# Attention backward on one Trainium2 core: the scores of the next step beside the dP pair, dV/dK quads that lag two units and dQ quads eight, in a fixed order

## The chip, the cores and the metric

The kernel runs on one core of one Trainium2 chip. The metric is the device time of the whole kernel in microseconds (us); each figure is the median of three or four runs of one version. "Unit" below means the smallest piece of the attention backward stage: 4 heads, 128 queries, 512 keys. The stage has 512 units. A "half step" handles two of the four heads. In the profiles PE is TensorE's matmuls, PEld its weight loads, DVE VectorE, ACT ScalarE, POOL GpSimd, and SPq the queue on which SyncE issues transfers. SBUF and PSUM are the on-chip memories; matmuls write to PSUM. "dsT" is the tile that holds dS transposed; "the ring" below is the cycle in which the dQ quads free a dsT buffer, transposes fill it, these free dS buffers for the next multiplies, and later dQ quads follow.

## The reference, cut to what matters

The program is one transformer block (adaLN conditioning, attention, squared-ReLU MLP), forward and backward, on 2048 tokens, 512 channels, 32 heads of 16 channels. Only this part and its derivative matter here:

```python
scores = jnp.einsum('bhqd,bhkd->bhqk', q, k) * Dh ** (-0.5)
p = _softmax(scores, axis=-1)
o = jnp.einsum('bhqk,bhkd->bhqd', p, v)
```

For the derivative, the kernel recomputes E = exp(scores), computes dP = dO V^T with the softmax correction folded into an extra row, multiplies dS = E * dP, and then accumulates dV from E, dK from dS, and dQ from dS transposed.

## The kernel before

Each head occupies 32 of the 128 partitions, so the score and dP matmuls (S and dP below) are **row-tiled**: a matmul uses 32 rows of the PE array at row position 0, 32, 64 or 96. The accumulating matmuls come as **quads**, one matmul per head, and are **column-tiled**: all 128 rows, 32 columns each (16 for dV).

```python
ework = ...tile_pool(name="phIe", bufs=3)
tpool = ...tile_pool(name="phIt", bufs=2)                 # dsT: dS transposed, one block of 4 units
psu = ...tile_pool(name="psIu", bufs=3, space=PSUM)       # S and dP share three buffers
psa = ...tile_pool(name="psIa", bufs=1, space=PSUM)

def score_pair(u, pair):
    ...
    if pair == 0:
        bst[u] = (ework.tile([P, 4, 512], BF, name="E_u", tag="E_u"),
                  ework.tile([P, 4, 512], BF, name="dS_u", tag="dS_u", bufs=4))
    E_u, dS_u = bst[u]
    psS = psu.tile([P, 2, 512], F32, name="psS_u", tag="pu")
    for hi in range(2):
        r = 32 * (2 * pair + hi)
        PE.matmul(psS[:, hi, :], ..., tile_position=(r, 0))               # S
    ACT.activation(E_u[:, 2 * pair:2 * pair + 2, :], psS[:], AF.Exp, scale=SCALE)
    psD = psu.tile([P, 2, 512], F32, name="psD_u", tag="pu")
    for hi in range(2):
        r = 32 * (2 * pair + hi)
        PE.matmul(psD[:, hi, :], ..., tile_position=(r, 0))               # dP
    DVE.tensor_tensor(dS_u[:, 2 * pair:2 * pair + 2, :], psD[:], E_u[...], ALU.mult)

def transpose_unit(u):
    if qi == 0:
        dqt[hg, qc, kc] = tpool.tile([P, 16, 512], BF, name="dsT", tag="dsT")
    SP.dma_start(out=dqt[hg, qc, kc][:, :, qi * P:(qi + 1) * P], in_=..., transpose=True)

def kv_quads(u): ...      # 4 matmuls with dS (dK), 4 with E (dV), into accVK
def dq_quad(b, kt): ...   # 4 matmuls with dsT, into dqacc; needs all four transposes of its block

LAG = 6
for u in range(NU + LAG + 4):
    if u < NU:
        ...                                   # load_head two blocks ahead
        score_pair(u, 0)
    if 1 <= u <= NU:
        kv_quads(u - 1)
    if u < NU:
        score_pair(u, 1)
        transpose_unit(u)
    v = u - LAG - 3
    if 0 <= v < NU:
        dq_quad((hg, qc, kc), qi)
```

The text of the loop is not the order that runs: a scheduler orders the instructions of each engine when the program is built.

## Time and profile before

| | before |
|---|---|
| whole kernel, median | 5007.97 us |
| attention backward, first exp to end of last dQ matmul | 2144 us |
| per unit | 4.19 us |
| granted TensorE clock in the stage | 0.61 |

The first view is the table of one stretch of time, here the stage. Its columns are the stretch, its length, then the busy time of each engine with the number of its instructions, the granted clock, the DMA share and GB/s.

```profile
core 0: us, PE busy (x) PEld busy (x) DVE busy (x) ACT busy (x) POOL busy (x), PEclk, DMA share, GB/s
2574.00:4720.00 2146.00, 1944.39 (x10234) 368.38 (x10233) 1222.26 (x1024) 1100.73 (x1185) 152.85 (x110) 0.61 0.73 136
```

PE is busy 91% of the stage, while DVE and ACT are busy 57% and 51%. One should not conclude that PE's arithmetic is the bound. The Trainium skill, "Trainium Kernel Development and Optimization", Performance Expectations, warns that matmul busy time is a bad metric for how close a kernel is to its roofline, because matmuls are pipelined.

The groups of instructions by line show the duration of one operation (second number) and how long its engine sat idle just before it, with what ended that idle time:

```profile
L716 DVE TENSOR_TENSOR dS_u<-psD_u,E_u 128x1024 bf16<-128x1024 f32 x1024 | 1222.3, 1222 | 965.6 <-ACT E_u L710 780.2
L710 ACT ACTIVATE E_u<-psS_u 128x1024 bf16<-128x1024 f32 x1024 | 1018.6, 1023 | 886.3 <-PE psS_u L708 881.4
...
L714 PE MATMUL psD_u<-iv,ido 32*128 32x512 bf16 x2048 | 643.3, 540 | 107.7 <-ACT E_u L710 91.9
...
L708 PE MATMUL psS_u<-ik,iq 32*128 32x512 bf16 x2048 | 601.6, 532 | 22.5 <-ACT E_u L710 14.8
...
L762 PE MATMUL dqacc<-dsT,KS_tok 128*32 128x512 bf16 x2048 | 427.9, 605 | 12.5 <-DMA dsT<-dS_u 9.8
```

ACT needs 2 x 1.02 us per unit and DVE 2 x 1.22 us, well under 4.19 us. ACT waits for scores, DVE waits for exp. The list of waits (who waited for whom, total us, times, longest) says the same for 2700 to 4700 us:

```profile
ACT E_u L710 <- PE psS_u L708: 829.6, 552, 3.4
DVE dS_u L716 <- ACT E_u L710: 683.0, 486, 3.2
```

The timeline shows how PE works at the low clock. Columns: start, duration, engine, line, operation, tiles, count, and in brackets the idle time before it and its releaser.

```profile
3405.05 0.61 PE L736 MATMUL accVK<-dS_u,qz_14655 128*32 128x512 bf16 x2
...
3405.60 0.60 PE L708 MATMUL psS_u<-ik,iq 32*128 32x512 bf16 x1
...
3406.13 0.61 PE L736 MATMUL accVK<-dS_u,qz_14655 128*32 128x512 bf16 x2
...
3406.14 1.03 PE L739 MATMUL accVK<-E_u,dOs_tok 128*16 128x512 bf16 x4
...
3407.10 0.60 PE L708 MATMUL psS_u<-ik,iq 32*128 32x512 bf16 x1
3407.10 1.02 PE L714 MATMUL psD_u<-iv,ido 32*128 32x512 bf16 x2
3407.74 1.02 ACT L710 ACTIVATE E_u<-psS_u 128x1024 bf16<-128x1024 f32 x1 [2.36 <-PE psS_u L708]
...
3408.06 0.61 PE L762 MATMUL dqacc<-dsT,KS_tok 128*32 128x512 bf16 x1
...
3408.60 0.61 PE L708 MATMUL psS_u<-ik,iq 32*128 32x512 bf16 x2
...
3408.79 1.23 DVE L716 TENSOR_TENSOR dS_u<-psD_u,E_u 128x1024 bf16<-128x1024 f32 x1 [1.94 <-ACT E_u L710]
```

Groups of one tiling kind start 0.54 us apart when they hold one set of matmuls (3405.05, 3405.60, 3406.13) and 0.96 us apart when they hold two serial sets (3406.14 to 3407.10). A lone score matmul at 3405.60 costs the same 0.54 us as a full set would. S and dP on the same row tiles need two sets (3407.10 to 3408.06). The Trainium skill, "TensorEngine Tiling (Array Packing)", Key Properties, says that changing the tiling mode drains TensorE; the trace agrees, with about 0.11 us per group beyond 0.43 us per set.

### The profile page before, as it was taken

What the parts mean: (1) busy time and instruction counts of PE and PEld (TensorE: products, weight loads), DVE (VectorE), ACT (ScalarE), POOL (GpSimd) and SP (SyncE); (2) the same over time, 40 slices, a digit from 0 to 9 for tenths busy, and PEclk for the clock granted to TensorE, in tenths of its full rate; (3) what the DMA queues carried; (4) which work ended last, traced back from release to release, by engine and by line L of the source; (5) the groups of instructions that cost most, each with busy time, mean ns of one, the idle gap of its engine ahead of it and who ended that gap; (6) DMA issues with size and microseconds to landing.
All of it is one profiled execution on the core that took longest, in us unless ns stands there. A gap on an engine that the chain in (4) does not pass through costs nothing.

```text
span 5010.0 us, 48266 instructions
## 1 busy us (share of the span) xinstructions
PE 4158.7 (83%) x18556; PEld 1052.9 (21%) x18629; DVE 2069.8 (41%) x3264; ACT 2232.8 (45%) x2462; POOL 274.0 (5%) x282
## 2 busy tenths in 40 slices
PE   4789999999997872866579999998989999989766
PEld 1222222222222321322221111111111111111122
DVE  7610000000004752720336555555555555555473
ACT  0058888888884000000025555545554554555411
POOL 2000000000000000001310000010000000000000
PEclk7865555555555886966855565666565655666687
DMA  3220000000001243365467867777686877677513
GB/s 110 82 79 9 9 1 9 9 9 8 2 1 42 110 129 90 89 204 173 133 148 132 159 127 150 128 134 143 125 153 123 153 124 147 127 134 130 123 56 92
DMA packets 1212437, 489.34 MB, mean 98 GB/s; under 512 B 1144611, under 2 KB 1174823, under 8 KB 1210669
## 3 DMA queue, kind: packets, MB, share of 16 engines
q1 hardware_dynamic: 1189550, 455.84, 41.5%
q0 software_dynamic: 6144, 28.32, 1.9%
q10 hardware_dynamic: 16512, 2.10, 0.3%
q8 instruction: 146, 2.39, 0.2%
q14 instruction: 85, 0.70, 0.0%
HBM read 124.35 MB, written 80.37 MB: 41 GB/s over the span
## 4 chain that ended last, share of the span: by engine, by line
PE 33%; ACT 8%; DVE 5%; DMA 3%; issue 3%; SPq 1%; POOL 0%; ACTq 0%; DVEq 0%; POOLq 0%
PE psS_u L708 8%; PE accVK L736 8%; ACT E_u L710 7%; PE psD_u L714 6%; PE dqacc L762 5%; PE accVK L739 4%; DVE dS_u L716 3%; DMA dsT<-dS_u 1%; SPq L919 1%; DMA stld<-stok_st 0%; DVE dh1acc L831 0%; DVE dqkv_tok L823 0%; DMA out_dram<-w2blk 0%; ACT vktmp L747 0%; POOL dOs_tokpad L595 0%
## 5 line engine op out<-in xcount | busy, mean ns | idle before, releaser
L716 DVE TENSOR_TENSOR dS_u<-psD_u,E_u 128x1024 bf16<-128x1024 f32 x1024 | 1222.3, 1222 | 965.6 <-ACT E_u L710 780.2
L710 ACT ACTIVATE E_u<-psS_u 128x1024 bf16<-128x1024 f32 x1024 | 1018.6, 1023 | 886.3 <-PE psS_u L708 881.4
L302 ACT ACTIVATE ET<-psST 128x1024 bf16<-128x1024 f32 x1024 | 1046.5, 1024 | 228.4 <-PE psST L299 226.3
L714 PE MATMUL psD_u<-iv,ido 32*128 32x512 bf16 x2048 | 643.3, 540 | 107.7 <-ACT E_u L710 91.9
L299 PE MATMUL psST<-qt_sb,kt_sb 32*128 32x512 bf16 x2048 | 658.3, 603 | 17.3 <-DMA kt_sb<-KtP 17.3
L306 PE MATMUL oacc<-ET,vaug 128*32 128x512 bf16 x2048 | 626.1, 604 | 45.9 <-ACT ET L302 4.5
L708 PE MATMUL psS_u<-ik,iq 32*128 32x512 bf16 x2048 | 601.6, 532 | 22.5 <-ACT E_u L710 14.8
L309 DVE COPY ostage<-oacc 128x512 f32<-128x512 f32 x32 | 22.1, 692 | 1083.7 <-PE oacc L306 1083.7
L739 PE MATMUL accVK<-E_u,dOs_tok 128*16 128x512 bf16 x2048 | 462.9, 554 | 0.0
L762 PE MATMUL dqacc<-dsT,KS_tok 128*32 128x512 bf16 x2048 | 427.9, 605 | 12.5 <-DMA dsT<-dS_u 9.8
L736 PE MATMUL accVK<-dS_u,qz_14655 128*32 128x512 bf16 x1024 | 316.8, 543 | 35.5 <-DVE dS_u L716 35.3
L736 PE MATMUL accVK<-dS_u,qz_14654 128*32 128x512 bf16 x1024 | 303.7, 557 | 26.8 <-DVE dS_u L716 26.7
L708 PEld LDWEIGHTS <-iq 32*128 32x128 bf16 x2048 | 126.1, 96 | 663.8 <-issue 650.3
L306 PEld LDWEIGHTS <-vaug 128*32 128x32 bf16 x2048 | 151.7, 102 | 466.1 <-issue 437.5
L570 ACT ACTIVATE w1blk<-aw_0_13090 128x512 bf16<-128x512 f32 x1 | 0.6, 597 | 556.2 <-PE aw_0_13090 L566 556.2
L748 POOL TENSOR_TENSOR dVKacc<-dVKacc,vktmp 128x512 f32<-128x512 f32 x96 | 121.3, 1264 | 1910.0 <-ACT vktmp L747 1910.0
L714 PEld LDWEIGHTS <-ido 32*128 32x128 bf16 x2048 | 144.2, 100 | 331.6 <-issue 309.3
L299 PEld LDWEIGHTS <-kt_sb 32*128 32x128 bf16 x2048 | 111.4, 99 | 478.0 <-issue 478.0
L490 PE MATMUL pds<-gfT,w2T 128*128 128x512 bf16 x219 | 54.4, 400 | 109.6 <-DVE dzT L493 79.5
L736 PEld LDWEIGHTS <-qz_14655 128*32 128x32 bf16 x1024 | 59.1, 99 | 312.4 <-issue 311.9
L736 PEld LDWEIGHTS <-qz_14654 128*32 128x32 bf16 x1024 | 56.1, 99 | 295.8 <-issue 295.8
L262 PE MATMUL ppad<-xn1T,wpadT 128*128 128x512 bf16 x376 | 99.1, 409 | 21.7 <-DVE stagep L265 16.2
(1253 smaller groups left out, 2931.6 us busy)
## 6 DMA issues: line engine op xcount, KB each, us to landing
dzld<-dztok_st POOLq DMA_DIRECT2D x32, 448.0 KB, 3.7
dzld<-dztok_st SPq DMA_DIRECT2D x32, 448.0 KB, 3.6
dsT<-dS_u SPq DMA_TRANSPOSE x512, 4.3
rT_st<-rT SPq DMA_DIRECT2D x4, 1792.0 KB
rtok_st<-rtok SPq DMA_DIRECT2D x16, 448.0 KB, 2.5
stok_st<-stok SPq DMA_DIRECT2D x16, 448.0 KB
rTb<-rT_st SPq DMA_DIRECT2D x4, 1792.0 KB
rtokb<-rtok_st SPq DMA_DIRECT2D x16, 448.0 KB, 4.0
```

Source lines behind the costliest of these rows:

```text
L262: PE.matmul(pp[:], wpadT[:, ic, which, hg, :], h1T[:, ic, qc * 512:(qc + 1) * 512], start=(ic == 0), stop=(ic == DC - 1))
L299: PE.matmul(ps[:, hi, :], kt_sb[32 * hq:32 * hq + 32, kt * P:(kt + 1) * P], qt_sb[32 * hq:32 * hq + 32, qc * 512:(qc + 1) * 512], start=Tr ...
L302: ACT.activation(ET[:, 2 * pair:2 * pair + 2, :], ps[:], AF.Exp, scale=SCALE)
L306: PE.matmul(oacc[32 * hq:32 * hq + 32, :], lhsT, ET[:, hq, :], start=(kt == 0), stop=(kt == TT - 1), tile_position=(0, 32 * hq), skip_grou ...
L708: PE.matmul(psS[:, hi, :], st["q"][r:r + 32, qt * P:(qt + 1) * P], st["k"][r:r + 32, kc * 512:kc * 512 + 512], start=True, stop=True, tile ...
L710: ACT.activation(E_u[:, 2 * pair:2 * pair + 2, :], psS[:], AF.Exp, scale=SCALE)
L714: PE.matmul(psD[:, hi, :], st["do"][r:r + 32, qt * P:(qt + 1) * P], st["v"][r:r + 32, kc * 512:kc * 512 + 512], start=True, stop=True, til ...
L716: DVE.tensor_tensor(dS_u[:, 2 * pair:2 * pair + 2, :], psD[:], E_u[:, 2 * pair:2 * pair + 2, :], ALU.mult)
L736: PE.matmul(acc[32 * hq:32 * hq + 32, :], st["qz"][:, qt, hq, :], dS_u[:, hq, :], start=(qi == 0), stop=False, tile_position=(0, 32 * hq), ...
L739: PE.matmul(acc[32 * hq:32 * hq + DH, :], dOs_tok[:, qt, (hg * 4 + hq) * DH:(hg * 4 + hq + 1) * DH], E_u[:, hq, :], start=False, stop=(qi ...
L748: POOL.tensor_tensor(dst, dst, tmp[:], ALU.add)
L762: PE.matmul(acc[32 * hq:32 * hq + 32, :], KS_tok[:, kc * 4 + kt, h * DH:h * DH + 32], tT[:, hq * 4 + kt, :], start=(kc == 0 and kt == 0), ...
```

## The change

Its intent: fix the instruction order of PE, ACT and DVE by hand. In each half step j, issue the scores S(j) next to dP(j-1), which sits on the other two row tiles, so that all four row tiles work at once; then one whole kind of quads. dV/dK quads lag two units, dQ quads eight (one and nine in the text before). A fourth E buffer pays for the longer lag.

```diff
-                bst[u] = (ework.tile([P, 4, 512], BF, name="E_u", tag="E_u"),
+                bst[u] = (ework.tile([P, 4, 512], BF, name="E_u", tag="E_u", bufs=4),
                           ework.tile([P, 4, 512], BF, name="dS_u", tag="dS_u", bufs=4))
 ...
             ACT.activation(E_u[:, 2 * pair:2 * pair + 2, :], psS[:], AF.Exp, scale=SCALE)
+
+        def dp_pair(u, pair):
 ...
             psD = psu.tile([P, 2, 512], F32, name="psD_u", tag="pu")
 ...
-        for u in range(NU + LAG + 4):
-            if u < NU:
-                ...
-                score_pair(u, 0)
-            if 1 <= u <= NU:
-                kv_quads(u - 1)
-            if u < NU:
-                score_pair(u, 1)
-                transpose_unit(u)
-            v = u - LAG - 3
-            if 0 <= v < NU:
-                hg, qc, kc, qi = units[v]
-                dq_quad((hg, qc, kc), qi)
+        with tc.manual_schedule(engines={PE.engine, ACT.engine, DVE.engine}):
+            for j in range(2 * NU + 18):
+                u = j // 2
+                if j < 2 * NU:
+                    ...
+                    score_pair(u, j % 2)
+                if 1 <= j <= 2 * NU:
+                    dp_pair((j - 1) // 2, (j - 1) % 2)
+                    if (j - 1) % 2 == 1:
+                        transpose_unit((j - 1) // 2)
+                if j % 2 == 0 and 2 <= u < NU + 2:
+                    kv_quads(u - 2)
+                v = u - 8
+                if j % 2 == 1 and 0 <= v < NU:
+                    hg, qc, kc, qi = units[v]
+                    dq_quad((hg, qc, kc), qi)
```

More of the change, by code (lines that the diff above doesn't have):

```diff
@@ L710, in score_pair @@
             ACT.activation(E_u[:, 2 * pair:2 * pair + 2, :], psS[:], AF.Exp, scale=SCALE)
+        def dp_pair(u, pair):
+            hg, qc, kc, qi = units[u]
+            st = hst[hg]
+            qt = qc * 4 + qi
+            E_u, dS_u = bst[u]
             psD = psu.tile([P, 2, 512], F32, name="psD_u", tag="pu")
@@ L770, in dq_quad @@
                         SP.dma_start(out=dQtP[hg], in_=hst[hg]["dq"][:])
-        LAG = 6
         NU = len(units)
         load_head(0)
-        for u in range(NU + LAG + 4):
-            if u < NU:
-                if units[u][1:] == (0, 2, 0) and units[u][0] + 1 < HG:
-                    load_head(units[u][0] + 1)
-                score_pair(u, 0)
-            if 1 <= u <= NU:
-                kv_quads(u - 1)
-            if u < NU:
-                score_pair(u, 1)
-                transpose_unit(u)
-            v = u - LAG - 3
-            if 0 <= v < NU:
-                hg, qc, kc, qi = units[v]
-                dq_quad((hg, qc, kc), qi)
+        with tc.manual_schedule(engines={PE.engine, ACT.engine, DVE.engine}):
+            for j in range(2 * NU + 18):
+                u = j // 2
+                if j < 2 * NU:
+                    if j % 2 == 0 and units[u][1:] == (0, 2, 0) and units[u][0] + 1 < HG:
+                        load_head(units[u][0] + 1)
+                    score_pair(u, j % 2)
[9 more added lines that the diff above has]
+                    dq_quad((hg, qc, kc), qi)
     qpool.release()
```

## The prediction

> **What bounds the kernel now.** The change touches only attention backward: by the timeline, 2574 us (first exp) to 4719 us (last dQ matmul), so 2146 of 5010 us for 512 units (4 heads x 128 queries x 512 keys), 4.19 us a unit. The table of that window shows PE busy 91%, DVE 57%, ACT 51%, DMA 73%, granted clock 0.61. No engine's own work fills a unit: ACT needs 2 x 1.02 us, DVE 2 x 1.22 us. The groups by line show ACT idle 881 us for the scores and DVE idle 780 us for exp: PE order and latency are the bound. By the timeline, at the low clock, a group of matmuls in one tiling mode costs about 0.11 us plus 0.43 us for each set that must follow another on the same tiles (0.54, 0.97, 1.40 us); at the full clock 0.33 us and 0.22 us for each more. I count 4.4 groups a unit, oddly cut: one quad matmul alone (0.54 to 0.76 us), single score matmuls, S and dP of one pair on the same row tiles (0.96 us). The Trainium skill, "TensorEngine Tiling (Array Packing)", Key Properties, says that a change of tiling mode drains TensorE; the 0.11 us agree.
>
> **What changes.** No operation is added or removed. The order becomes fixed: per half unit S(j), dP(j-1) on the other two row tiles, then whole quads (eight dV/dK, or four dQ). Groups per unit: exactly 4; serial sets fall from 7 to 5 where S and dP overlap. That four row tiles can share a set is suggested by three-matmul groups of 0.53 us. PE work: 3 x 0.54 + 0.97 = 2.6 us a unit at the low clock, 1.55 us at the full one.
>
> **New critical chain.** There are three score/dP buffers in PSUM, so dP(j) needs the one that exp(j) empties. Over two half steps: S to exp 0.63, exp 1.02, wait 0.1, dP 0.54, dV/dK quads 0.97 = 3.25 us a unit; with the accumulator copies on ACT (0.60 us each four units, partly exposed) 3.3 us at the low clock. At the full clock the chain is 0.42 + 1.02 + 0.1 + 0.33 + 0.55 = 2.4 us, and other floors win: DVE 2.3 to 2.45 us; the DMA transpose, 2.6 us when several queue up (packets in the trace), with the head loads and stores (3 MB each 64 units) about 2.8 us; and the ring dQ -> dsT buffer free -> transpose (4.3 us to landing) -> dS buffer free -> multiply -> S -> next block's dQ, about 11.4 us per four units. So 2.85 us a unit. The clock should be mixed, as before or somewhat higher (denser array use): mean 3.1 us. 512 x 3.1 + 25 us of start and drain = 1610 us, against 2146: about 530 us saved. The other 2864 us are untouched.
>
> **Prediction: 4480 us, 8 in 10 within 4350 to 4620.** Faster by over 2%: 0.95; within 2%: 0.03; slower: 0.02.
>
> **Right if** the profile shows: the stage lasting 1480 to 1750 us; S and dP pairs in one 0.54 us set when exp is done in time; DVE 75 to 85% and DMA over 90% busy; DVE waits on transposes; no change before 2574 us. **Wrong if:** S and dP don't overlap, because exp(j-1) ends after S(j) has gone (the stage stays near 3.3 us even with the clock up); the clock falls to 0.5 throughout (about 4580 us); the ring of two dsT and four dS buffers stalls the fixed order, which can't fill holes as the old order could (over 3.5 us a unit); or the clock rises to near full and DMA alone sets 2.75 us (about 4300 us).

## More of the kernel before

The SP queue, which issues the transposes, waits for nothing but the multiplies that feed it:

```profile
SPq L722 <- DVE dS_u L716: 1320.3, 408, 6.4
```

## The result, and the profile after

The changed kernel takes 4602.43 us (4596.18 to 4605.47, four runs) against 5009.94 us for the kernel before, in the same rounds. The ratio is 0.9185, 95% interval 0.9163 to 0.9207. Ratios here are the mean time of one kernel's fast runs over that of the other's fast runs of the same rounds, so they are not quite the ratio of the medians that are quoted. The stage took 1752 us, 3.42 us a unit; nearly all that was saved was saved there (392 us of 407; the stage also began 14 us earlier in this profile, see below).

```profile
core 0: us, PE busy (x) PEld busy (x) DVE busy (x) ACT busy (x) POOL busy (x), PEclk, DMA share, GB/s
2574.00:4305.00 1731.00, 1602.53 (x10162) 306.54 (x10159) 1212.08 (x1016) 1113.25 (x1174) 154.92 (x111) 0.53 0.92 167
```

The share of PE is 93%, and the clock fell from 0.61 to 0.53. The DMA share adds up the times of packets and is no share of a limit: it is 0.92 here and 1.15 in two versions below. The groups that answer to those of before:

```profile
L722 DVE TENSOR_TENSOR dS_u<-psD_u,E_u 128x1024 bf16<-128x1024 f32 x1024 | 1221.8, 1221 | 566.2 <-DMA dsT<-dS_u 284.1
L710 ACT ACTIVATE E_u<-psS_u 128x1024 bf16<-128x1024 f32 x1024 | 1045.5, 1024 | 544.4 <-PE psD_u L720 428.4
...
L720 PE MATMUL psD_u<-iv,ido 32*128 32x512 bf16 x2048 | 608.9, 583 | 81.6 <-DVE dS_u L722 65.8
...
L708 PE MATMUL psS_u<-ik,iq 32*128 32x512 bf16 x2048 | 606.1, 587 | 52.7 <-DVE dS_u L722 37.6
...
L768 PE MATMUL dqacc<-dsT,KS_tok 128*32 128x512 bf16 x2048 | 309.2, 595 | 8.8 <-DMA dsT<-dS_u 8.8
```

The operations have their old durations, and the idle time of DVE fell from 966 to 566 us. The new releaser of DVE is the transpose:

```profile
ACT E_u L710 <- PE psD_u L720: 396.9, 365, 5.4
...
DVE dS_u L722 <- DMA dsT<-dS_u: 269.3, 158, 5.6
DVE dS_u L722 <- PE psD_u L720: 152.0, 299, 2.0
```

The timeline of one unit at the low clock:

```profile
3404.23 0.61 PE L708 MATMUL psS_u<-ik,iq 32*128 32x512 bf16 x2
...
3404.42 0.61 PE L720 MATMUL psD_u<-iv,ido 32*128 32x512 bf16 x2
3404.88 1.02 ACT L710 ACTIVATE E_u<-psS_u 128x1024 bf16<-128x1024 f32 x1 [0.51 <-PE psS_u L708]
...
3404.96 0.62 PE L768 MATMUL dqacc<-dsT,KS_tok 128*32 128x512 bf16 x4
...
3405.51 0.61 PE L708 MATMUL psS_u<-ik,iq 32*128 32x512 bf16 x2
...
3405.95 0.61 PE L720 MATMUL psD_u<-iv,ido 32*128 32x512 bf16 x2
...
3406.15 1.02 ACT L710 ACTIVATE E_u<-psS_u 128x1024 bf16<-128x1024 f32 x1 [0.25 <-PE psS_u L708]
...
3406.49 0.62 PE L742 MATMUL accVK<-dS_u,qz_14655 128*32 128x512 bf16 x4
...
3406.89 0.65 PE L745 MATMUL accVK<-E_u,dOs_tok 128*16 128x512 bf16 x4
...
3407.47 0.60 PE L708 MATMUL psS_u<-ik,iq 32*128 32x512 bf16 x2
```

Follow the loop. S starts at 3404.23; exp starts 0.65 us later and runs to 3405.90; dP of that pair, which must take the PSUM buffer that this exp empties, starts at 3405.95, 0.44 us after the next S at 3405.51; the dV/dK quads start at 3406.49 and the next S at 3407.47. That is 3.24 us, against 3.25 us in the prediction. In the other half step (3407.47) S and dP do start together and share a set.

The SP queue now waits a second way:

```profile
SPq L728 <- DVE dS_u L722: 620.8, 364, 3.5
SPq L728 <- PE psD_u L720: 532.9, 123, 6.4
```

The second line names psD_u, but by the built program what the transposes wait for on PE is the dQ quads (the trace agrees: in the median the first transpose of a block is issued 0.04 us after the end of the last of them): the first transpose of every block needs the dsT buffer that the dQ quads of two blocks before have to release. There were 123 such waits among the 128 blocks, 533 us in all. Transposes that were issued at once before (median 0.03 us after their multiply) are now issued 4.7 to 6.1 us after it.

### The profile page after: what moved, and what is told of

It is laid out like the page before. It is cut to its first block, busy times and chain, and to the rows that moved or that the text cites. A ratio compares the mean times of both kernels' runs of the same rounds, so it can differ in the third digit from the quotient of the medians.

```text
span 4603.7 us, 48383 instructions
## 1 busy us (share of the span) xinstructions
PE 3821.1 (83%) x18556; PEld 991.7 (22%) x18629; DVE 2070.6 (45%) x3264; ACT 2256.5 (49%) x2462; POOL 274.6 (6%) x282
## 4 chain that ended last, share of the span: by engine, by line
PE 26%; DMA 13%; DVE 5%; issue 3%; ACT 2%; SPq 1%; POOL 0%; DVEq 0%; ACTq 0%; POOLq 0%
DMA dsT<-dS_u 10%; PE psS_u L708 8%; PE psD_u L720 4%; PE dqacc L768 4%; PE accVK L742 4%; PE accVK L745 3%; DVE dS_u L722 2%; ACT E_u L710 1%; SPq L927 1%; DMA stld<-stok_st 1%; DVE dh1acc L839 0%; DVE dqkv_tok L831 0%; DMA out_dram<-w2blk 0%; DMA iqs<-q_st 0%; POOL dOs_tokpad L595 0%
## 5 line engine op out<-in xcount | busy, mean ns | idle before, releaser
L710 ACT ACTIVATE E_u<-psS_u 128x1024 bf16<-128x1024 f32 x1024 | 1045.5, 1024 | 544.4 <-PE psD_u L720 428.4
L720 PE MATMUL psD_u<-iv,ido 32*128 32x512 bf16 x2048 | 608.9, 583 | 81.6 <-DVE dS_u L722 65.8
L745 PE MATMUL accVK<-E_u,dOs_tok 128*16 128x512 bf16 x2048 | 321.9, 617 | 0.0
L768 PE MATMUL dqacc<-dsT,KS_tok 128*32 128x512 bf16 x2048 | 309.2, 595 | 8.8 <-DMA dsT<-dS_u 8.8
L720 PEld LDWEIGHTS <-ido 32*128 32x128 bf16 x2048 | 165.7, 99 | 320.9 <-issue 311.6
L742 PE MATMUL accVK<-dS_u,qz_14654 128*32 128x512 bf16 x1024 | 155.0, 595 | 0.0
L742 PE MATMUL accVK<-dS_u,qz_14655 128*32 128x512 bf16 x1024 | 154.8, 593 | 0.2 <-DVE dS_u L722 0.2
L768 PEld LDWEIGHTS <-KS_tok 128*32 128x32 bf16 x2048 | 57.3, 101 | 224.8 <-issue 224.4
```

Source lines behind the costliest of these rows:

```text
L720: PE.matmul(psD[:, hi, :], st["do"][r:r + 32, qt * P:(qt + 1) * P], st["v"][r:r + 32, kc * 512:kc * 512 + 512], start=True, stop=True, til ...
L742: PE.matmul(acc[32 * hq:32 * hq + 32, :], st["qz"][:, qt, hq, :], dS_u[:, hq, :], start=(qi == 0), stop=False, tile_position=(0, 32 * hq), ...
L745: PE.matmul(acc[32 * hq:32 * hq + DH, :], dOs_tok[:, qt, (hg * 4 + hq) * DH:(hg * 4 + hq + 1) * DH], E_u[:, hq, :], start=False, stop=(qi ...
L768: PE.matmul(acc[32 * hq:32 * hq + 32, :], KS_tok[:, kc * 4 + kt, h * DH:h * DH + 32], tT[:, hq * 4 + kt, :], start=(kc == 0 and kt == 0), ...
```

## The experiments

Three chips were used, with the kernel before run beside each version, so versions of different calls are compared by their ratios to it. All versions give correct results. The table gives, for each, the median time, the ratio, and from its profile the stage time per unit with head loads included, the median unit (over blocks of four), and the mean granted clock of the stage.

| version | median us | ratio | stage/512 | median unit | clock |
|---|---|---|---|---|---|
| before | 5007.97 | 1 | 4.19 | 4.29 | 0.61 |
| ebufs | 5011.92 | 1.0001 | 4.21 | 4.29 | 0.60 |
| nolook | 4886.18 | 0.9765 | 3.97 | 3.86 | 0.50 |
| nolookring3 | 4636.32 | 0.9253 | 3.48 | 3.45 | 0.50 |
| dq2 | 4612.44 | 0.9214 | 3.44 | 3.33 | 0.80 |
| **the change** | 4602.43 | 0.9185 | 3.42 | 3.30 | 0.53 |
| samering3 | 4532.38 | 0.9050 | 3.27 | 3.24 | 0.50 |
| ring3 | 4526.86 | 0.9048 | 3.27 | 3.24 | 0.50 |
| freering3 | 4520.43 | 0.9027 | 3.25 | 3.24 | 0.52 |
| free | 4469.27 | 0.8926 | 3.17 | 3.03 | 0.75 |
| swap | 4432.60 | 0.8862 | 3.11 | 3.01 | 0.72 |
| dq2ring3 | 4317.27 | 0.8614 | 2.85 | 2.71 | 0.90 |
| dq2swapring3 | 4310.54 | 0.8607 | 2.84 | 2.74 | 0.91 |
| swapring3 | 4290.92 | 0.8567 | 2.80 | 2.72 | 0.82 |

Theory A was that the loop on PE just followed (S, exp, dP, dV/dK quads, next S) sets the time at the low clock. Rival B was that the ring of transposes and their buffers sets it. Theory C came later: that the clock is a result of the order of the quads, and decides between the two.

### ring3: a third transpose buffer

A plain third buffer did not fit in SBUF (it did not build: the pool after it needs 20 KB per partition, and 9 were left), so the third buffer is a tile that is needed only after the stage; it is saved to DRAM and loaded back.

```diff
+        SP.dma_start(out=dx1_st[:], in_=g_tok[:])          # before the stage
-                dqt[hg, qc, kc] = tpool.tile([P, 16, 512], BF, name="dsT", tag="dsT")
+                dqt[hg, qc, kc] = g_tok if (u // 4) % 3 == 2 else tpool.tile([P, 16, 512], BF, name="dsT", tag="dsT")
+        SP.dma_start(out=g_tok[:], in_=dx1_st[:])          # after the stage
```

> The changed kernel with a third dsT buffer (a tile that is saved to DRAM before the stage and loaded back after it; results stay correct), so that a transpose needn't wait for the dQ quads of two blocks before. Theory A (the loop on PE at the low clock, S to exp to dP to dV/dK quads to the next S, 3.25 us a unit): the steady unit stays at 3.25 to 3.35 us, total within 1% of the changed kernel (4560 to 4620 us), though the wait of DVE for transposes falls by more than half. Rival B (the ring of transpose buffers and the DMA set the 3.33 us): the unit falls to 3.0 us or below, total 4450 us or less.

Measured: 4526.86 us, ratio 0.9048, 1.5% under the changed kernel's 0.9185. This falls between the two expectations: below theory A's 4560 to 4620 us, above rival B's 4450, with a steady unit as theory A had it. The waits on the ring are nearly gone, both on the SP queue (2574 to 4300 us) and on DVE (2700 to 4000 us; under the third buffer's name, g_tok, another 4.6 us):

```profile
SPq L729 <- DVE dS_u L723: 1268.9, 508, 4.4
```

```profile
DVE dS_u L723 <- PE psD_u L721: 299.7, 747, 0.8
...
DVE dS_u L723 <- DMA dsT<-dS_u: 6.8, 7, 2.1
```

The stage row of the table of stretches (columns as before) and the timeline:

```profile
2574.00:4200.00 1626.00, 1607.28 (x10008) 278.01 (x10008) 1226.16 (x1003) 1100.70 (x1159) 151.13 (x108) 0.50 0.97 176
```

```profile
3302.09 0.60 PE L709 MATMUL psS_u<-ik,iq 32*128 32x512 bf16 x2
...
3302.76 2.10 ACT L711 ACTIVATE E_u<-psS_u 128x1024 bf16<-128x1024 f32 x2
...
3303.18 0.60 PE L709 MATMUL psS_u<-ik,iq 32*128 32x512 bf16 x2
...
3303.83 0.61 PE L721 MATMUL psD_u<-iv,ido 32*128 32x512 bf16 x2
...
3304.37 0.62 PE L743 MATMUL accVK<-dS_u,qz 128*32 128x512 bf16 x4
...
3304.77 0.64 PE L746 MATMUL accVK<-E_u,dOs_tok 128*16 128x512 bf16 x4
...
3305.34 0.10 PEld L709 LDWEIGHTS <-iq 32*128 32x128 bf16 x2 [0.85 <-issue]
```

S at 3302.09 to the next S of that parity at 3305.34 is 3.25 us, and 87% of the blocks of the stage are within 0.03 us of 3.24 us a unit. With the clock at 0.50 (two windows of the stage apart), this is theory A's loop; the mean of 3.27 us comes from the few other blocks. What the ring had added to the changed kernel was 0.15 us a unit (3.42 less 3.27), or some 79 us.

### swap: dV/dK and dQ quads change places in every second unit

```diff
-                if j % 2 == 0 and 2 <= u < NU + 2:
+                if j % 2 == u % 2 and 2 <= u < NU + 2:
                     kv_quads(u - 2)
                 v = u - 8
-                if j % 2 == 1 and 0 <= v < NU:
+                if j % 2 != u % 2 and 0 <= v < NU:
```

> The changed kernel with the dV/dK quads and the dQ quads changing places in every second unit, so that the heavy quads fall by turns on both half-step loops. Theory A: the two loops, 3.25 and 2.80 us a unit, become equal at about 3.0 us; total 4440 to 4500 us if nothing else holds, 4500 to 4540 if the transposes begin to hold. Rival B: no change beyond 1%, as neither the transposes nor their buffers change.

Measured: 4432.60 us, ratio 0.8862, 3.5% better than the change and a little below theory A's range. But the edit turned out not to be a clean test. It did three things: it equalised the two PE loops; it put two groups of eight dV/dK matmuls into consecutive half steps, and the clock rose to 0.72; and, which I had overlooked when I wrote that buffers do not change, it issues the last dQ quads of a block half a step earlier and so frees the buffer earlier: transposes were issued 3.7 to 4.9 us after their multiply here, where the changed kernel had 4.7 to 6.1 us.

### nolook and nolookring3: the fixed order without the lookahead

```diff
-                if 1 <= j <= 2 * NU:
-                    dp_pair((j - 1) // 2, (j - 1) % 2)
-                    if (j - 1) % 2 == 1:
-                        transpose_unit((j - 1) // 2)
+                    dp_pair(u, j % 2)
+                    if j % 2 == 1:
+                        transpose_unit(u)
```

The edit stands within the block that runs for j below twice the number of units. S and dP of the same pair then always share row tiles.

> The fixed order kept, but dP(j) follows S(j) of the same pair in the same half step, so S and dP always share row tiles: no pairing on other tiles, no score ahead. If the fixed order with whole quads is most of the gain: PE work 2 x 0.97 + 0.97 + 0.54 = 3.45 us a unit, so 3.5 to 3.65 us, total 4650 to 4730 us. If the pairing on other row tiles is most of it: 4.0 us a unit or more, total over 4900 us.

Measured: 4886.18 us, ratio 0.9765, between the two expectations. So I ran it again with the third buffer:

> The fixed order without lookahead (S and dP of the same pair on the same row tiles) with the third dsT buffer. If only the buffer ring made that order slow (transposes were issued 6 to 8 us after their multiply): 3.45 to 3.6 us a unit, total 4630 to 4720 us. If the missing lookahead itself costs it: within 1.5% of nolook, 4810 us or more.

Measured: 4636.32 us, ratio 0.9253, as the first expectation had it: only the ring had made that order slow. The stage row:

```profile
2574.00:4330.00 1756.00, 1753.71 (x10148) 297.00 (x10140) 1245.02 (x1018) 1119.49 (x1176) 152.93 (x109) 0.50 0.90 165
```

The unit is 3.45 us, exactly PE's summed work (2 x 0.97 + 0.97 + 0.54). So whole quads in a fixed order, with the lags and the E buffer of the change, give much of the gain even without lookahead, once the buffers are out of the way. (The kernel before was not run with a third buffer, but its transposes never waited for one.) The lookahead is worth 0.21 us a unit beyond that (3.45 to 3.24). With two buffers the ring cost the order without lookahead 0.49 us a unit (3.97 less 3.48), and the order with it 0.15.

### samering3: S and dP on the same row tiles in every second half step

```diff
-                    score_pair(u, j % 2)
+                    score_pair(u, (j + u) % 2)
-                    dp_pair((j - 1) // 2, (j - 1) % 2)
+                    dp_pair((j - 1) // 2, (j - 1 + (j - 1) // 2) % 2)
```

(on ring3; E_u and dS_u are then allocated at whichever pair comes first)

> The ring3 kernel with the two pairs of every second unit in reversed order, so that in the half steps with the dV/dK quads S and dP fall on the same row tiles, and nothing else moves. In these steps dP waits for exp anyway, about 0.44 us after S in the trace. Theory A: 3.24 to 3.30 us a unit, total 4515 to 4560 us. If the concurrency of other row tiles is what the gain rests on there: 0.43 us a unit more, 4720 us or more.

Measured: 4532.38 us, ratio 0.9050 against 0.9048. In the half steps where dP waits for exp, the other row tiles are worth nothing: the S set is over by the time dP may start. The pairing pays in the other half steps only.

### ebufs, free and freering3: is it the fixed order?

ebufs is the kernel before with the fourth E buffer alone (`bufs=4` on E_u). free is the changed text with the manual schedule taken away:

```diff
-        with tc.manual_schedule(engines={PE.engine, ACT.engine, DVE.engine}):
+        with ExitStack():
```

> The kernel before with only the fourth E buffer. If buffers gave a part of the gain: 4800 to 4950 us. If lookahead is needed first (my expectation): within 1% of the kernel before, 4960 to 5050 us.

> The changed program text (scores one half step ahead, four E buffers, the lags) but without the fixed order, so the scheduler orders PE, ACT and DVE again. If the fixed order is what counts: near the kernel before, 4850 to 5010 us. If the lookahead and buffers are what counts: within 2% of the changed kernel, 4510 to 4690 us.

Measured: ebufs 5011.92 us, ratio 1.0001, so the buffer alone does nothing. free 4469.27 us, ratio 0.8926: **faster** than the fixed order by 2.8% (0.8926 over 0.9185), better than either expectation allowed. The lookahead, the lags and the buffer in the text, taken together, are enough for the gain (no run takes them apart under the scheduler); fixing the order by hand cost some of it. Its stage row:

```profile
2574.00:4150.00 1576.00, 1403.10 (x10018) 337.29 (x10016) 1192.39 (x1003) 1095.26 (x1160) 148.56 (x107) 0.76 0.99 181
```

With the third buffer:

> The changed text without the fixed order and with the third dsT buffer. If the scheduler's order is held by the same two things, buffers and clock: 2.7 to 2.95 us a unit, total 4270 to 4400 us, within 2% of the kernel with swapped quads and three buffers. If its advantage over the changed kernel came from using the two buffers better: less gain than 2% over the 4469 us without the third buffer, 4400 us or more.

Measured: 4520.43 us, ratio 0.9027, slower than free without the buffer, and equal to ring3. By its number the second expectation holds, but neither had foreseen a loss of 1.1%. The row says why:

```profile
2574.00:4200.00 1626.00, 1596.51 (x10057) 282.05 (x10055) 1230.34 (x1009) 1103.82 (x1166) 147.42 (x107) 0.52 0.97 176
```

With the waits on the ring gone, the scheduler's kernel settled into the same even rhythm as ring3, at 3.24 us a unit and a clock of 0.52 instead of 0.75. A wait less, and the kernel is slower: this made the clock the suspect.

### dq2ring3 and dq2: more work on purpose

In all these traces the granted clock is either 0.5 or 1.0. I counted the quad matmuls that start in each of its windows of 3.41 us, in the windows at the low clock. In the kernel before, windows that were followed by the full clock held 14.0 quad matmuls on average (82 windows), the others 9.1 (412 windows). The changed kernel's regular order gives mostly 12 a window, and it went up only 11 times. So I issued each dQ quad twice, on a K with half the scale, which leaves the result correct:

```diff
-    DVE.tensor_scalar(KS_tok[:], KS_tok[:], SCALE, None, ALU.mult)
+    DVE.tensor_scalar(KS_tok[:], KS_tok[:], SCALE / 2, None, ALU.mult)
-            for hq in range(4):
+            for hh in range(8):
+                hq = hh % 4
```

> The ring3 kernel with more work on purpose: each dQ quad is issued twice on a K that carries half the scale, so the result stays correct. Both half-step loops then have eight quad matmuls (0.97 us) and PE has 3.03 us of work a unit at the low clock. Theory A alone: the loop is unchanged, 3.24 us a unit, clock 0.50, total 4510 to 4550 us. Theory C (the clock follows how densely quads fill a window of 3.4 us: in the traces the clock goes up after windows with 13 to 16 quad matmuls, where this order gives 12): with 16 a window the clock rises above 0.6 and the kernel becomes faster in spite of the added work, 2.85 to 3.1 us a unit, total 4330 to 4450 us.

Measured: 4317.27 us, ratio 0.8614, a little below theory C's range: 2048 matmuls more, and 4.8% less time than ring3 (0.8614 over 0.9048). The stage row, to be compared with that of ring3:

```profile
2574.00:4010.00 1436.00, 1232.42 (x12206) 316.46 (x12209) 1200.84 (x1020) 1094.92 (x1177) 153.00 (x109) 0.91 1.15 202
```

The clock rose from 0.50 to 0.91 and PE's busy share fell from 99% to 86%, with 20% more matmuls. Then the same without the third buffer:

> The doubled dQ quads alone, on the changed kernel with its two dsT buffers. Theory C: the clock of the stage rises from 0.53 to 0.7 or more and the kernel gets faster although PE has more work; the buffer ring then holds it where the prediction put the full-clock case, 2.85 to 3.1 us a unit, total 4340 to 4470 us. If the clock matters only together with the third buffer: within 1% of the changed kernel (4560 to 4650 us).

Measured: 4612.44 us, ratio 0.9214, not faster at all. The first expectation failed in its time, though not in its clock:

```profile
2574.00:4300.00 1726.00, 1353.65 (x12094) 317.54 (x12093) 1198.39 (x1011) 1099.58 (x1169) 152.48 (x109) 0.80 0.93 167
```

```profile
DVE dS_u L722 <- DMA dsT<-dS_u: 324.0, 160, 7.2
```

The clock is 0.80, and DVE waits 324 us in total for transposes between 2700 and 4200 us. So the two causes are joined. With this way of raising the clock, either alone is worth little, both together are worth 6%:

| ratio to before | clock low | clock raised by doubled dQ |
|---|---|---|
| two dsT buffers | 0.9185 (the change) | 0.9214 (dq2) |
| three dsT buffers | 0.9048 (ring3) | 0.8614 (dq2ring3) |

The right column also has the added work of the doubled quads, so it is not the clock alone. swap, with two buffers, no added work and a clock of 0.72, gained 3.5%, but it frees the buffer earlier as well.

The trace shows where the ring's time goes. I took medians over the blocks, in us from the end of the last dQ quad of two blocks before, which is what frees the buffer when there are two:

```
                  transposes of the block       the multiplies that reuse   last dQ quad of
                  issue   last packets          their dS buffers start      the block before starts
the change         0.04    3.8  6.3  9.0 11.9   4.6  7.2 10.2 13.2          12.6
dq2 (clock 0.80)   0.04    3.8  6.4  9.0 12.2   4.6  7.2 10.4 13.4          12.8
ring3             -7.2    -3.4 -0.2  3.1  6.4   2.8  6.1  9.3 12.6          12.4
```

With two buffers the first transpose is issued 0.04 us after its buffer is free, and the multiplies follow the transposes, 2.5 to 3.2 us apart, at either clock. In the changed kernel 80%, 73%, 64% and 10% of the four multiplies began within 1.0 us of the last packet of the transpose whose dS buffer they reuse; in dq2 it was 76%, 70%, 52% and 40%; in ring3 1%, 0%, 1% and 4%. The lag of the dQ quads and the number of dS buffers stand in the same ring; no run changed either of them, so a third dsT buffer is one way out of it and perhaps not the only one.

### swapring3 and dq2swapring3: what both together give

> Both edits together: quads that change places in every second unit, and the third dsT buffer. Theory A (PE loops) with the buffers out of the way: 3.02 us a unit at the low clock; at the higher clock only the transposes hold it (2.6 us back to back, more with the head loads). With a clock of 0.6 to 0.75 in the stage: 2.8 to 2.95 us, total 4310 to 4400 us. If the swapped kernel was already held by the DMA: no more than 1% better than swap alone (4390 to 4440 us).

Measured: 4290.92 us, ratio 0.8567, below the expected range. **This version beats both kernels**, by 14.3% and 6.7% (0.8567 over 0.9185), without added work. It differs from ring3 only in the places of the quads, and its clock is 0.82 where ring3 has 0.50: order alone can raise the clock.

```profile
2574.00:3990.00 1416.00, 1241.87 (x10178) 320.33 (x10174) 1192.12 (x1018) 1104.08 (x1175) 156.35 (x111) 0.83 1.15 206
```

> All three edits: swapped quads, doubled dQ quads, third buffer. The unit should be at the floor of the transposes, 2.6 to 2.7 us between the head loads: 4270 to 4310 us, within 1% of the version with two edits. If PE is still a part of the bound, the clock near 1 would bring it below 4250 us.

Measured: 4310.54 us, ratio 0.8607, half a per cent slower than without the doubled quads and just at the upper end of the range. Raising the clock further (0.91) gives nothing more. All three versions with three buffers and a raised clock have a median unit of 2.71 to 2.74 us, near the transpose, whose packets take 2.5 to 2.6 us from first to last (medians of these traces), and which lands every 2.5 us when several run back to back; with head loads on the same DMA engines the mean is 2.80 to 2.85 us. That the DMA is the floor here is a reading of these numbers; no run took the transposes away.

## Why the prediction was right or wrong

The time, 4602 us, lies within 4350 to 4620 us, near its end. The gain was 407 us where about 530 us were forecast. That the range holds it is partly luck: it was wide enough for a risk that the central sum had not counted on.

- **Right: which chain.** "S to exp 0.63, exp 1.02, wait 0.1, dP 0.54, dV/dK quads 0.97 = 3.25 us a unit" is what the trace shows (3.24 us), and ring3, where nothing else holds, has 3.24 us through nearly the whole stage.
- **Right: about 3.3 us a unit at the low clock.** The median unit was 3.30 us; 3.42 us with the head loads.
- **Wrong: "The clock should be mixed, as before or somewhat higher (denser array use): mean 3.1 us."** This is the term that was mis-sized. The clock was 0.53 and the mean unit 3.42 us; the stage took 1752 us where the sum had 1610, and the total missed by 122 us. The prediction named the case among its risks ("the clock falls to 0.5 throughout (about 4580 us)") and that is nearly what happened. Denser use did not bring a higher clock here: a regular order with mostly 12 quad matmuls a window had it low, and the same order with the dQ quads doubled had it at 0.80 (dq2).
- **Wrong, and hidden by the first error: "So 2.85 us a unit" at the full clock.** dq2 has a clock of 0.80 and 3.44 us. The ring was put at "about 11.4 us per four units", where dq2 shows 13.4 us. The sum let only the first transpose of a block hold a multiply; the trace shows two or three of the four multiplies usually held, each by its own transpose, 2.5 us apart or more. So in this order a clock of 0.80 did not shorten the unit. dq2 is not a clean test of it, since its PE has more work; and swap and free, with two buffers and clocks of 0.72 and 0.75, have 3.11 and 3.17 us, close to the 3.1 us of the sum. Only with the third buffer are 2.85 us reached (dq2ring3, clock 0.90); there the ring holds less, and I take the floor to be the transposes, which no run tested.
- **Partly right: the overlap of S and dP.** It occurs in one of two half steps; in the other dP waits for exp, and samering3 shows that the row tiles do not matter there.
- **Signs that were named:** the stage in 1480 to 1750 us (1752, just missed), DMA over 90% (92%, right), waits of DVE on transposes (right), DVE 75 to 85% (70%, missed), no change before 2574 us (the stage began 14 us earlier in this profile; the same front part began anywhere between 2558 and 2575 us in the other profiles).
- **Not foreseen:** that the order need not be fixed by hand for the gain. The same text under the scheduler is 2.8% faster with two buffers and equal with three (0.9027 and 0.9048). Why the scheduler's order keeps the clock up with two buffers and not with three was not settled.

What stays open: the rule by which the clock rises. Doubled quads raised it, and so did moving them (swapring3). But free went up after 52 windows with only 12.2 quad matmuls on average, and of the 73 low windows of ring3 that held 16 a single one was followed by the full clock. So the count in a window is not the rule.

## What to carry to other kernels

When a loop on one engine and a ring of buffers have nearly the same period, removing either can show almost nothing; test both removed together before calling one harmless. Read the granted clock of the stage beside every PE duration, and do not assume that busier means faster clocked: compare orders; where the clock is stuck at half, as in ring3, other places for the same matmuls (swapring3), or even added ones (dq2ring3), are worth a try. Before fixing an order by hand, run the same text under the scheduler, and count how often each in-order queue will wait for a buffer that a later instruction frees.

## What the Trainium skill lacked or had wrong

- "TensorE: Matmul & The Clock Gate", Part 1, What's actually happening: the two states and the window are confirmed (only 0.5 and 1.0 occur; all stretches but the cut last one are multiples of 3413 ns). Its condition for the full clock, a busy window of about 3.4 us, is not enough if busy is what the profile counts as busy (it models the ends of matmuls): ring3 had PE busy 99% of 1626 us, and the clock was full in a single window of 3.4 us.
- The same page lacks that more matmuls of column tiles in a window can raise the clock and shorten the run: 0.50 to 0.90 and 4527 to 4317 us from 2048 redundant matmuls; nor that the places of the same matmuls can do it (0.50 to 0.82, ring3 to swapring3).
- "TensorEngine Tiling (Array Packing)", Key Properties, says that a mode change drains TensorE but gives no price: about 0.11 us per group at the low clock.
- "DMA: Bandwidth & Descriptors", Where 436 GB/s comes from, has the fabric at 435 GB/s bind an SBUF to SBUF transpose. The transposes of 512 KB here took 2.5 to 2.6 us back to back, some 200 to 210 GB/s (524288 bytes over that time), so something else bound them. Its table of measured facts is nearer, with 261 GB/s for a transpose that has a non-contiguous middle dimension; the runs stay below that too.
